# A written-out order for every instruction and place, and stacked one-pass state products for half of w_in

## The chip, the cores and the metric

The kernel runs on one core of one Trainium2 chip. The metric is the device time of one execution in microseconds (us); a smaller number is better. The core has five engines with their own queues, each of which works strictly in order: TensorE (PE; its weight loads are shown apart as PEld), VectorE (DVE), ScalarE (ACT), GpSimd (POOL) and SyncE (SP), which here only issues transfers. Matmul results land in PSUM, which has 8 banks of 128 x 512 float32; everything else lives in SBUF, or in DRAM.

## The reference

Eight batches (B) of 8 heads (H), 512 tokens (S), 32 state rows (NS), 64 columns per head (D). First a two-way attention between tokens and state, then a two-layer network with softplus over all rows of all batches (512 + 32 rows per batch, 512 model columns, 2048 hidden columns).

```python
scores = scale * np.matmul(x, state.transpose(0, 1, 3, 2))
a = softmax(scores)                 # with 1e-09 added to the sum
xread = np.matmul(a, state)
scores2 = scale * np.matmul(state, x.transpose(0, 1, 3, 2))
a2 = softmax(scores2)
sread = np.matmul(a2, x)
rows = np.concatenate([xread, sread], axis=2)     # heads side by side: 4608 rows of 512
...
h = rows @ w_in                     # 512 x 2048
g = np.maximum(h, 0.0) + np.log1p(np.exp(-np.abs(h)))
out = g @ w_out                     # 2048 x 512
```

w_in and w_out are float64; x, state and the output are float32.

## The kernel before

**Numbers in parts.** TensorE multiplies float32 in full, or float32r in one pass with fewer bits. Where the kernel uses float32r it splits a value into a high part (a cast, `split` L101, line L105 on ScalarE or L98 on GpSimd) and a low part (value minus high part, L106, on VectorE or GpSimd) and adds three products (PASSES: high x high, high x low, low x high). The float64 weights arrive as 64-bit words and are put together to float32 by `as_f32` (L120): a scaling of the upper words on ScalarE or GpSimd (L129 to L136), shifts of the lower words on VectorE (L131, or the 16-bit pair L140 and L141), and a join on VectorE (L142).

**The xread rows** are never formed. Since xread @ w_in = a @ (state @ w_in), the kernel multiplies the state of each batch with w_in first. w_in is cut into four quarters c of 512 hidden columns. This state product is V; V of one batch and quarter is 128 x 2 x 512. It is made in two ways:

- For batches 0 to 3 by `make_v0` (quarter 0, in 8 pieces of 256 columns) and `make_vf` (quarters 1 to 3, four pieces q of 512 columns each). Two float32 matmuls per piece, one with QZ[0] (batches 0 and 1; L185, L227) and one with QZ[1] (batches 2 and 3; L194, L238). The result for batches 0 and 1 is copied into SBUF tiles Vf (L232, L234); the one for batches 2 and 3 goes through a tile ve to DRAM (Vd[0, c]).
- For batches 4 to 7 by `make_v`: the converted w_in, which was stored to DRAM (wsc), is read back piece by piece; `head` (L271) stacks the high part of the 64 rows of a head over their low part into one 128 x 512 tile R; `product` (L259, matmuls in L262) multiplies it with the high and the low state parts (StK), two one-pass matmuls for the four batches at once. The result goes to DRAM (Vd[1, c], one page per head).

**The main loop.** A slot (b, ft) is batch b and hidden block ft of 128 columns, 16 per batch. `gemm1` (L506) makes h for it with six matmuls of 512 columns (L513) from V and the attention weights aT; `softplus` (L498) applies softplus on ScalarE (L500) and splits the result into ghi and glo; `gemm2` (L517) adds 4 x 3 matmuls (L520) into four accumulator banks. Every quarter of V is split before its use (`split_v`). Batches 0 and 1 take turns by quarters of ft (0: block 0 to 3; 1: 0 to 7; 0: 4 to 11; 1: 8 to 15; 0: 12 to 15), with partial sums kept in SBUF in between (L609, L612), so that work can begin before all of w_in and w_out is there. Then come batches 2 to 6, the state rows of all batches (`gemm1_read`, L560, from sreadT and w_in read back from DRAM), and batch 7.

**Attention** (`attention`) is a generator with one step per letter: scores (Q: L369 in float32 for batches 0 and 1, L375 for the others), VectorE's 32 x 32 transpose and the softmax over the state rows (A, M, m, N, D), the softmax over the tokens (E, e), the transposes on TensorE (G, L425), the reads (R: L443, L449), and the gathering into sr (X, L465 to L469).

**The order** is written by hand: LOADS for the first transfers, the strings START, BLOCK, BLOCK2, BLOCK3 and LAST for everything behind, one letter per step (`run`, L638): a bar is a gemm1 slot, g a gemm2, p a split of V, F a fetch of V, v, V and U a step of the three ways to make V, W a w_out block, a to c a step of attention. MOVED is a set of steps that run on another engine than usual; most of them are casts and differences that go to GpSimd. Tiles come from pools with a tag and a number of buffers; PSUM is divided into 2 banks "aux", 2 "h", 4 "acc".

All transfers are issued on SP's queue in the order of the program.

Of the kernel before, what the change touches and what calls it, by code (L numbers as in the profile page):

```python
# [49 lines left out]
def attention_then_softplus_mlp(ctx: ExitStack, tc, xn, xt, zq, zp, stk, w_in, w_out, out):  # L50
    nc = tc.nc
    nc.scalar.preload_act_table_set("natural_log_exp_and_others")

    cp = ctx.enter_context(tc.tile_pool(name="cp", bufs=1))
    sp = ctx.enter_context(tc.tile_pool(name="sp", bufs=1))
    dp = ctx.enter_context(tc.tile_pool(name="dp", bufs=1, space=DRAM))
    ps = ctx.enter_context(tc.tile_pool(name="ps", bufs=1, space=PSUM))
    uid = [0]

    def sb(tag, shape, dt=F32, bufs=1):  # L60
        uid[0] += 1
        return sp.tile(shape, dt, tag=tag, name=f"{tag}_{uid[0]}", bufs=bufs)

    def bank(tag, bufs):
        uid[0] += 1
        return ps.tile([P, 512], F32, tag=tag, name=f"{tag}_{uid[0]}", bufs=bufs)

    BANKS = {"aux": 2, "h": 2, "acc": 4}
    turn = cycle(("h", "acc", "acc"))
    early = [True]  # L70

    def aux():
        if early[0]:
            tag = next(turn)
            return bank(tag, BANKS[tag])
        return bank("aux", 2)

    ident = cp.tile([P, P], F32, name="ident")
    make_identity(nc, ident)


    if WARM:
        idle = sb("sr", [P, P], bufs=2)
        nc.vector.memset(idle, 0.0)
        pb = aux()
        for _ in range(WARM):
            nc.tensor.matmul(pb[:, 0:P], idle, idle, start=True, stop=True)

    def rouse():
        pb = aux()  # L90
        for c in range(4):
            nc.tensor.transpose(pb[:, P * c:P * c + P], ident, ident)

    def vec(*what):
        return nc.gpsimd if what in MOVED else nc.vector

    def pool_copy(dst, src):
        nc.gpsimd.tensor_scalar(dst, src, 1.0, 0.0, ALU.mult, ALU.add)  # L98


    def split(hi, lo, src, *what):  # L101
        if ("hi",) + what in MOVED:
            pool_copy(hi, src)
        else:
            nc.scalar.copy(hi, src)  # L105
        vec(*what).tensor_tensor(lo, src, f32(hi), ALU.subtract)  # L106

    def load_w(src, tag=None):
        w64 = src.dtype == I64
        tag = tag or ("k4" if w64 else "wt")  # L110
        t = sb(tag, src.shape, I64 if w64 else F32, bufs=K4 if tag == "k4" else 2)
        nc.sync.dma_start(t, src)
        return t

    def as_f32(t, *what, tag="wt"):  # L120
        if t.dtype != I64:
            return t
        v = t.bitcast(I32).rearrange("p (n t) -> p n t", t=2)
        lo, hi = v[:, :, 0], v[:, :, 1]
        n = t.shape[1]
        h2 = sb("k2", [P, n], bufs=K2)
        r = sb(tag, [P, n], bufs=2 if tag == "wt" else 1)
        if early[0] or ("pre",) + what in MOVED:
            nc.scalar.activation(h2, f32(hi), AF.Prelu, scale=2.0 ** -112, alpha=-(2.0 ** 32))  # L129
            u = r.bitcast(I32)  # L130
            nc.vector.tensor_scalar(u, lo, 29, None, ALU.logical_shift_right)  # L131
        else:
            if ("h2",) + what in MOVED:
                nc.gpsimd.tensor_scalar(h2, f32(hi), 2.0 ** -112, 0.0, ALU.mult, ALU.add)
            else:
# [205 lines left out]

# [404 lines left out]
```

## Time and profile before

| | |
|---|---|
| median of 3 runs | 697.95 us (695.63 to 699.69) |
| span of the profiled execution | 695.4 us |
| TensorE busy | 675.9 us, 3028 matmul records |
| VectorE busy | 395.0 us, 692 instructions |
| ScalarE busy | 390.9 us, 661 instructions |
| GpSimd busy | 218.4 us, 209 instructions |
| moved by DMA | 82.90 MB, mean 119 GB/s |

Engines are named PE, PEld, DVE, ACT, POOL and SP (SPq: its queue); L12 is line 12 of the kernel. In the view of groups, a row gives line, engine, operation, what is written from what, the matmul's shape of weights and of moving data, how many records; then busy time in us, mean ns of one, and the idle time just before them with what ended it. In the view by stretches, each engine has its busy time and the number of its instructions, followed by the granted TensorE clock, the share of the 16 DMA engines in use, and GB/s. In the timeline, a row begins with its start and its length in us; a row x12 is twelve instructions merged. A float32 matmul leaves two records, a one-pass one leaves one. In the view of transfers, the last number is the median time in us from issue to landing.

### The profile page before, as it was taken

To read this page: it belongs to the slowest core of one execution; us is meant where nothing else is said; L and a number is where in the kernel's file an instruction comes from. 1 tells how busy PE (TensorE), PEld (TensorE's weight loads), DVE (VectorE), ACT (ScalarE), POOL (GpSimd) and SP (SyncE) were. 2 spreads that over 40 slices of the span, in tenths; PEclk is the share of its full clock that TensorE was granted. 3 is DMA by queue.
4 is the path that set the end of the run, shared out by engine and by line. 5 is a ranking of instruction groups with operands and counts; after the bars stand their busy time and mean duration, and the time that the engine had idled before them with its cause. 6 is when DMAs were issued, how large, how long until landed. Compare 5 with 4: busy or idle time off the path is not lost.

```text
span 695.4 us, 8922 instructions
## 1 busy us (share of the span) xinstructions
PE 675.9 (97%) x3028; PEld 540.1 (78%) x3028; DVE 395.0 (57%) x692; ACT 390.9 (56%) x661; POOL 218.4 (31%) x209
## 2 busy tenths in 40 slices
PE   7879999999999999999999999999999999999997
PEld 4456667788887877888888888888888889988886
DVE  5898788319777885776556752676257423311101
ACT  4787975434848944775538634863386334423321
POOL 0130157146433584156222450235022400121310
PEclk9999999999999999999999999999999999999999
DMA  7778895103253545464423220321121113512001
GB/s 253 258 258 293 307 301 188 49 0 122 68 167 122 184 156 166 143 199 136 134 94 121 69 90 31 107 76 31 31 69 45 40 39 98 168 30 61 1 0 61
DMA packets 42061, 82.90 MB, mean 119 GB/s; under 512 B 6176, under 2 KB 13088, under 8 KB 42016
## 3 DMA queue, kind: packets, MB, share of 16 engines
q1 hardware_dynamic: 42016, 82.33, 36.1%
q8 instruction: 24, 0.39, 0.2%
q14 instruction: 21, 0.17, 0.1%
HBM read 56.62 MB, written 25.69 MB: 118 GB/s over the span
## 4 chain that ended last, share of the span: by engine, by line
PE 83%; ACT 7%; DVE 5%; DMA 2%; issue 1%; POOL 1%; SPq 0%; POOLq 0%; DVEq 0%; ACTq 0%
PE acc L520 49%; PE h L513 22%; PE h L560 3%; PE aux L262 2%; PE aux L449 2%; PE aux L375 1%; ACT L500 1%; DMA xT<-in_xt_dram 1%; ACT t L500 1%; PE aux L425 1%; PE aux L238 1%; PE aux L227 1%; DMA k<-in_w_in_dram 1%; ACT ghi L105 1%; DVE glo L106 1%
## 5 line engine op out<-in xcount | busy, mean ns | idle before, releaser
L520 PE MATMUL acc<-wout,ghi 128*128 128x512 f32 x1088 | 341.7, 395 | 3.9 <-POOL wout L98 2.8
L520 PEld LDWEIGHTS acc<-wout,ghi 128*128 128x128 f32 x1088 | 203.8, 189 | 50.7 <-issue 3.6
L520 PE MATMUL acc<-wout,glo 128*128 128x512 f32 x544 | 214.2, 394 | 0.0
L513 PE MATMUL h<-aT,vhl 128*128 128x512 f32 x768 | 199.4, 398 | 0.1
L513 PEld LDWEIGHTS h<-aT,vhl 128*128 128x128 f32 x768 | 142.1, 188 | 35.3 <-issue 3.4
L500 ACT ACTIVATE t<-h 128x512 f32<-128x512 f32 x136 | 81.0, 598 | 121.4 <-PE h L513 81.1
L106 DVE TENSOR_TENSOR glo<-t,ghi 128x512 fp32r<-128x512 f32 x83 | 63.7, 770 | 124.2 <-ACT ghi L105 83.9
L106 POOL TENSOR_TENSOR glo<-t,ghi 128x512 fp32r<-128x512 f32 x53 | 70.9, 1338 | 159.5 <-ACT ghi L105 156.7
L520 PEld LDWEIGHTS acc<-wout,glo 128*128 128x128 f32 x544 | 102.4, 188 | 23.0 <-issue 0.7
L105 ACT CAST ghi<-t 128x512 fp32r<-128x512 f32 x96 | 59.1, 618 | 76.1 <-PE acc L520 75.6
L106 DVE TENSOR_TENSOR vhl<-vf,vhl 128x512 fp32r<-128x512 f32 x57 | 41.5, 728 | 58.6 <-ACT vhl L105 48.4
L98 POOL TENSOR_SCALAR ghi<-t 128x512 fp32r<-128x512 f32 x40 | 28.7, 718 | 82.1 <-PE acc L520 39.5
L105 ACT CAST vhl<-vf 128x512 fp32r<-128x512 f32 x60 | 37.1, 618 | 17.3 <-PE h L513 11.3
L500 ACT ACT_TABLE_LOAD x23 | 29.5, 1283 | 7.8 <-DVE glo L106 5.7
L380 DVE TENSOR_TENSOR sc<-aux,k 64x512 f32<-64x512 f32 x24 | 16.4, 683 | 23.4 <-ACT k L379 23.1
L98 POOL TENSOR_SCALAR vhl<-vf 128x512 fp32r<-128x512 f32 x12 | 8.4, 696 | 66.8 <-PE h L513 50.7
L277 DVE TENSOR_TENSOR R<-wt,R 64x512 fp32r<-64x512 f32 x23 | 18.8, 819 | 10.4 <-ACT R L276 7.3
L560 PEld LDWEIGHTS h<-sreadT,vhl 128*128 128x128 f32 x192 | 24.1, 191 | 0.6
L560 PE MATMUL h<-sreadT,vhl 128*128 128x256 f32 x192 | 24.3, 283 | 0.0
L106 POOL TENSOR_TENSOR vhl<-vf,vhl 128x512 fp32r<-128x512 f32 x15 | 21.9, 1457 | 6.4 <-ACT vhl L105 6.0
L262 PE MATMUL aux<-R,StK 128*128 128x512 f32 x64 | 19.1, 398 | 1.2 <-POOL R L277 0.7
L398 POOL TENSOR_TENSOR T<-T,mx 128x512 f32<-128x512 f32 x7 | 7.7, 1106 | 37.3 <-DVE mx L397 17.4
(156 smaller groups left out, 736.3 us busy)
## 6 DMA issues: line engine op xcount, KB each, us to landing
vd<-ve SPq DMA_DIRECT2D x44, 256.0 KB, 2.7
xT<-in_xt_dram SPq DMA_DIRECT2D x16, 512.0 KB, 3.7
k<-in_w_out_dram SPq DMA_DIRECT2D x16, 512.0 KB, 5.1
x<-in_xn_dram SPq DMA_DIRECT2D x16, 512.0 KB, 3.5
vf<-vd SPq DMA_DIRECT2D x64, 128.0 KB, 2.6
k<-in_w_in_dram SPq DMA_DIRECT2D x12, 512.0 KB, 4.9
out_dram<-o SPq DMA_DIRECT2D x24, 256.0 KB, 2.2
vf<-vd SPq DMA_DIRECT2D x16, 256.0 KB, 4.0
```

The lines of the kernel that those rows point to most:

```text
L98: nc.gpsimd.tensor_scalar(dst, src, 1.0, 0.0, ALU.mult, ALU.add)
L105: nc.scalar.copy(hi, src)
L106: vec(*what).tensor_tensor(lo, src, f32(hi), ALU.subtract)
L262: nc.tensor.matmul(pb, StK[i][:, h, :], r, start=(i == 0), stop=(i == 1))
L277: vec("R", *what, o).tensor_tensor(r[z], wf[a], f32(r[a]), ALU.subtract)
L380: nc.vector.tensor_tensor(sc[64 * j:64 * j + 64], pb[0:64], s2, ALU.add)
L398: vec("tmul", bk, g).tensor_tensor(T, T, sm.unsqueeze(2).broadcast_to([P, 16, NS]), ALU.mult)
L449: nc.tensor.matmul(pb[:, 256 * j:256 * j + 256], a2T[:, c, j].rearrange("p i n -> p (i n)"), v["xs"][j][:, c].rearrange("p i n -> p (i n)" ...
L500: nc.scalar.activation(t, h, AF.Softplus)
L513: nc.tensor.matmul(h, Vhl[b, ft // 2][:, vi, g, cs], aT[b][:, ai, g], start=(n == 0), stop=(n == 5))
L520: nc.tensor.matmul(acc[c], g[gi][:, c0:c0 + P], wout[ft][:, wi], start=(ft == first and i == 0), stop=(ft == last and i == 2))
L560: nc.tensor.matmul(h[:, 256 * i:256 * i + 256], Whl[u, i][:, wi, kt, :], sreadT[:, si, kt, :], start=(n == 0), stop=(n == 11))
```

## The change

The generators, the order strings and MOVED are replaced. A function `graph` now names every step of the kernel as an operation with its inputs, its outputs and the engines that may run it; the string PLAN lists all 2638 steps in one order, each as name, engine and buffer numbers. T is TensorE, A ScalarE, V VectorE, G GpSimd, S an issue on SP's queue; C and W are the second forms of the two conversion steps (C: the plain scaling on ScalarE; W: the pair of 16-bit shifts on VectorE). A buffer number is a place in SBUF (69 places of 2 KB per partition, and a few of 4 KB) or one of the 8 PSUM banks, without fixed roles. Every engine gets its steps in the order of PLAN.

```diff
+TURNS = ((0, 0, 4), (1, 0, 8), (0, 4, 12), (1, 8, 16), (0, 12, 16))
+PACKED = (2, 3)
+
+PLAN = """
+Lz.0:S:0 Lt.0.1.0:S:1 Lt.0.1.1:S:2 zn.0:G:3 Li.0.1:S:4 Li.0.0:S:5 Lq.1:S:6 Lq.0:S:7 Li.0.6:S:8 Lt.0.0.0:S:9 zc.0.0:V: zc.0.1:V: Lt.0.0.1:S:10
...
+gl.0.1:V:24 m.0.0.2:T:1 wh.3:A:36 wl.2:V:20 m.0.1.0:T: gl.0.2:V:37 m.0.1.1:T: wl.3:V:28 m.0.2.0:T: m.1.1:A: gl.0.3:V:30 m.1.0:A: m.0.2.1:T: N.1.1:V:
...
+P.1.2.0:T:2 o.1.0.0:V:9 Sp.0.2.5:S: P.1.2.2:T:3 pe.1.2.0:V:25 m.1.7.3:T: pe.1.2.2:V:5 Sp.1.2.0:S: P.0.2.0:T:0 o.1.0.3:V:48 P.0.2.1:T:2 Sp.1.2.2:S:
...
+So.7.2:S: o.7.0.3:A:63 So.7.3:S:
+"""
...
+    def stack(c, h, o, src, tok):
+        a, z = slice(64 * o, 64 * o + 64), slice(64 - 64 * o, 128 - 64 * o)
+        R = f"R.{c}.{h}"
+        op(f"Rh.{c}.{h}", "AG", [tok], [f"{R}:h"], lambda e: copy(e, r(at(R)[a]), at(src)[a]))
+        op(f"Rl.{c}.{h}", "VG", [tok, f"{R}:h"], [f"{R}:l"],
+           lambda e: eng(e).tensor_tensor(r(at(R)[z]), at(src)[a], at(R)[a], ALU.subtract))
+        for s4 in range(2) if c in PACKED else (1,):
+            k = f"{s4}.{c}.{h}"
+
+            def product(e, k=k, s4=s4):
+                for i, s in enumerate(("KH", "KL")):
+                    mm(at(f"pp.{k}"), r(page(f"{s}.{s4}.{h // 4}", 4, P)[:, h % 4]), r(at(R)), i == 0, i == 1)
+
+            op(f"P.{k}", "T", [f"KH.{s4}.{h // 4}", f"KL.{s4}.{h // 4}", f"{R}:h", f"{R}:l"], [f"pp.{k}"], product)
+            op(f"pe.{k}", "AV", [f"pp.{k}"], [f"px.{k}"], lambda e, k=k: copy(e, at(f"px.{k}"), at(f"pp.{k}")))
+            store(f"Sp.{k}", [f"px.{k}"], lambda s4=s4: io.Vd[s4, c][h], lambda k=k: at(f"px.{k}"), [f"D:vd.{k}"])
...
+            if c in PACKED:
+                for o in range(2):
+                    stack(c, 2 * q + o, o, f"wf.{k}", wf)
+                continue
+            for z in range(2):
+                op(f"V{z}.{k}", "T", [f"QZ.{z}", wf], [f"vp.{z}.{k}"],
+                   lambda e, z=z, k=k, q=q, n=n: mm(at(f"vp.{z}.{k}")[:, 0:n], page(f"QZ.{z}", 4, P)[:, q],
+                                                    page(f"wf.{k}", n), True, True))
...
+                kept = b < WHOLE and c not in PACKED
...
+                    n = 4 if b >= 4 or c in PACKED else 2
...
+    with tc.manual_schedule():
...
+        ops = graph(io, at, nc)
+        for step in PLAN.split():
+            name, e, where = step.split(":")
+            step = ops.pop(name)
+            where = [int(w) for w in where.split(",") if w]
+            for buf in step.places():
+                if buf not in place:
+                    put(buf, where.pop(0))
+            assert not where
+            step.emit(e)
+        assert not ops
```

Three things differ in what is done, beside order and places:

- **State products of quarters 2 and 3.** For the quarters in PACKED the float32 products with QZ are gone. The stacks R (`stack`: Rh, Rl) are made from the converted piece directly, and for each head the product P is made twice, with the state of batches 0 to 3 (s4 = 0) and of batches 4 to 7 (s4 = 1). Both results are copied (pe), stored to DRAM (Sp), and fetched (F) by all eight batches; batches 0 and 1 no longer keep V of these quarters in SBUF. Two more pieces of the stacked state (Lk) are loaded and split (kh, kl). Quarters 0 and 1 are made as before.
- **Engines.** In PLAN, GpSimd has two steps (zn, a memset each). All casts are on ScalarE, all differences on VectorE.
- **Transfers.** V is fetched by half quarters (256 columns), in pieces of 64 KB, or 128 KB where batches 2 and 3 read quarters 0 and 1; xT is loaded in two pieces per group. There are 466 issues in PLAN.

Names of steps in PLAN used below: V0 and V1 are the float32 products with QZ, h.b.ft is a gemm1, m.b.ft.c one accumulator's share of a gemm2, P.s4.c.h a stacked product, Q the scores, G and T transposes, R.b.g the reads.

More of the change, by code (lines that the diff above doesn't have):

```diff
@@ L1 @@
 from contextlib import ExitStack
-from itertools import cycle
 import concourse.bass as bass
@@ new lines, in width, with rounded @@
+def width(buf):
+    kind, *at = buf.split(".")
+    whole = at and at[0] in map(str, range(WHOLE))
+    if kind in ("vp", "pp", "qp", "gp", "rp", "tp", "h", "acc") or kind == "sc" and whole:
+        return 0
+    if kind in ("o8", "x", "xs", "Wf", "Vk"):
+        return 2
+    return 2 if kind == "w8" and at[0] != "0" or kind == "aa" and not whole else 1
+def rounded(buf):
+    kind, *at = buf.split(".")
+    return kind in ("KH", "KL", "R", "Vh", "Vl", "aH", "aL", "xh", "xl", "xs", "Wh", "Wl", "gH", "gL", "uH", "uL") \
+        or kind in ("z", "aa") and int(at[0]) >= WHOLE
@@ L49, in attention_then_softplus_mlp @@
+SMALL = {"mx": 16, "sm": 16, "nm": 1, "rs": 1, "rj": 2}
+class IO:
+    pass
 @with_exitstack
@@ L68, in attention_then_softplus_mlp @@
[L68 to L76, printed above, removed]
-    ident = cp.tile([P, P], F32, name="ident")
[L79 to L85, printed above, removed]
-        for _ in range(WARM):
-            nc.tensor.matmul(pb[:, 0:P], idle, idle, start=True, stop=True)
@@ L89, in rouse @@
[L89 to L106, printed above, removed]
@@ L492, in split_wout @@
-    def split_wout(ft):
-        assert ft < NFT - 1 or all(made[0, c] == 3 for c in range(1, 4))
-        wout[ft] = sb(f"wout{ft}", [P, 2, DM], F32R)
-        w = as_f32(ahead("out"), ft)
-        split(wout[ft][:, 0], wout[ft][:, 1], w, "wout", ft)
-    def softplus(h, *what):
-        t = sb("t", [P, 512], bufs=2)
-        nc.scalar.activation(t, h, AF.Softplus)
-        ghi = sb("ghi", [P, 512], F32R, bufs=3)
-        glo = sb("glo", [P, 512], F32R, bufs=3)
-        split(ghi, glo, t, "g", *what)
-        return ghi, glo
@@ L506, in gemm1 @@
-    def gemm1(b, ft):
-        h = bank("h", 2)
-        n = 0
-        cs = slice(P * (ft % 2), P * (ft % 2) + P)
-        assert made["aT", b] == 2
-        for g in range(2):
-            for vi, ai in PASSES:
-                nc.tensor.matmul(h, Vhl[b, ft // 2][:, vi, g, cs], aT[b][:, ai, g], start=(n == 0), stop=(n == 5))
-                n += 1
-        return softplus(h, min(b, 4), ft)
-    def gemm2(acc, g, ft, cols, first=0, last=NFT - 1):
-        for c, c0 in enumerate(cols):
-            for i, (gi, wi) in enumerate(PASSES):
-                nc.tensor.matmul(acc[c], g[gi][:, c0:c0 + P], wout[ft][:, wi],
-                                 start=(ft == first and i == 0), stop=(ft == last and i == 2))
@@ L523, in store @@
-    def store(acc, dsts, tags="oooo"):
-        for a, d, tag in zip(acc, dsts, tags):
-            o = sb(tag, [P, DM], F32, bufs=2)
-            evac(o, a)
-            if len(d.shape) == 2:
-                nc.sync.dma_start(d, o)
-            else:
-                for i in range(4):
-                    nc.sync.dma_start(d[i], o[32 * i:32 * i + 32])
-    def chain(*gens):
-        for f in gens:
-            yield from f()
-    wv = [w.rearrange("(g j o d) f -> j d g o f", g=2, j=2, o=2) for w in wsc]
@@ L553, in gemm1_read @@
-    def gemm1_read(u):
-        assert made["read"] == B
-        h = bank("h", 2)
-        for i in range(2):
-            n = 0
-            for kt in range(4):
-                for wi, si in PASSES:
-                    nc.tensor.matmul(h[:, 256 * i:256 * i + 256], Whl[u, i][:, wi, kt, :], sreadT[:, si, kt, :],
-                                     start=(n == 0), stop=(n == 11))
-                    n += 1
-        return softplus(h, B, u)
-    COLS = [0, P, 2 * P, 3 * P]
-    QTR = NFT // 4
@@ L670, in attention_then_softplus_mlp @@
-    v0 = make_v0()
-    v_first = make_vf(range(1, 4))
-    v_second = chain(prep_stk, lambda: make_v(range(4), 2))
-    att[0] = attention(0, ATT[0])
-    n = 0
-    for what, i in LOADS:
-        if what == "w":
-            src = w_in[0, n % 4][:, 256 * (n // 4):256 * (n // 4) + 256]
-            first.append(load_w(src, ("k4", "k4", "R", "o")[n // 2]))
-            n += 1
-        elif what == "q":
-            nc.sync.dma_start(QZ[i], zq[:, i])
-        elif what == "z":
-            load_z(0)
-        else:
-            load_xT(0, i)
@@ L686, in attention_then_softplus_mlp @@
-    run(START)
-    assert made["read"] == 3
-    for b in range(2, B - 1):
-        run({2: BLOCK2, 3: BLOCK3}.get(b, BLOCK), b)
-    run("|gFp" * (NFT // 2))
-    run(LAST)
-    while pend:
-        flush(True)
+    io = IO()
+    io.xn, io.xt, io.zq, io.zp, io.stk, io.w_in, io.w_out, io.out = xn, xt, zq, zp, stk, w_in, w_out, out
+    io.wsc = [dp.tile([DM, 512], F32, tag=f"wsc{c}", name=f"wsc{c}") for c in range(4)]
+    io.Vd = {}
+    for c in range(4):
+        io.Vd[0, c] = dp.tile([H, P, 512] if c in PACKED else [P, 4, 512], F32, tag=f"vd0_{c}", name=f"vd0_{c}")
+        io.Vd[1, c] = dp.tile([H, P, 512], F32, tag=f"vd1_{c}", name=f"vd1_{c}")
@@ new lines, in attention_then_softplus_mlp, with put @@
+    ident = cp.tile([P, P], F32, name="ident")
+    sreadT = cp.tile([P, 2, 4, B * NS], F32R, name="sreadT")
+    fixed = {"ident": ident, "sreadT": sreadT.bitcast(F32)}
+    for n, w in SMALL.items():
+        t = cp.tile([P, 2 * B, w], F32, name=n)
+        for b in range(B):
+            for g in range(2):
+                fixed[f"{n}.{b}.{g}"] = t[:, 2 * b + g, :]
+    place = {}
+    def put(buf, i):
+        n = width(buf)
+        if n == 0:
+            place[buf] = ps.tile([P, 512], F32, tag=f"bank{i}", name=buf.replace(".", "_"), bufs=1)
+        else:
+            t = sp.tile([P, 512 * n], F32R if rounded(buf) else F32, tag=f"{'sd'[n - 1]}{i}", name=buf.replace(".", "_"), bufs=1)
+            place[buf] = t.bitcast(F32) if rounded(buf) else t
@@ new lines, in at @@
+    def at(buf):
+        return fixed[buf] if buf in fixed else place[buf]
+    with tc.manual_schedule():
+        make_identity(nc, ident)
+        put("idle", 0)
+        put("h.idle", 0)
+        nc.vector.memset(at("idle")[:, 0:P], 0.0)
+        for _ in range(WARM):
+            nc.tensor.matmul(at("h.idle")[:, 0:P], at("idle")[:, 0:P], at("idle")[:, 0:P], start=True, stop=True)
+        ops = graph(io, at, nc)
[9 more added lines that the diff above has]
+        assert not ops
```

1009 lines of the change are left out of this document (556 added, 453 removed).

## The prediction

> **What bounds the kernel now.** I read the page first, then the busy time by stretch, then the TensorE groups, then single stretches of the timeline for the time from one instruction to the next.
>
> ```profile
> span 695.4 us, 8922 instructions
> ...
> PE 675.9 (97%) x3028; PEld 540.1 (78%) x3028; DVE 395.0 (57%) x692; ACT 390.9 (56%) x661; POOL 218.4 (31%) x209
> ...
> PE 83%; ACT 7%; DVE 5%; DMA 2%; issue 1%; POOL 1%; SPq 0%; POOLq 0%; DVEq 0%; ACTq 0%
> ```
>
> TensorE is the bound. But a busy PE is not a PE at its peak: matmuls overlap, so I count its work by the time from one start to the next.
>
> ```profile
> 675.29 16.33 PE acc L520 x72
> ...
> 589.75 2.87 PE h L560 x24
> ```
>
> ```profile
> 84.28 1.02 PE L227 MATMUL aux<-wt,QZ 128*128 128x512 f32 x2
> 85.14 1.02 PE L238 MATMUL aux<-wt,wout 128*128 128x512 f32 x2
> 85.60 1.03 PE L520 MATMUL acc<-wout,ghi 128*128 128x512 f32 x2
> 86.46 0.40 PE L520 MATMUL acc<-wout,glo 128*128 128x512 f32 x1
> ```
>
> A one-pass 512-column matmul (float32r) takes 16.33 / 72 = 0.227 us. A full float32 one is two records; from 84.28 to 86.46 there are two of them and two one-pass matmuls, so one takes (2.18 - 0.45) / 2 = 0.863 us, 3.8 times as much.
>
> ```profile
> L520 PE MATMUL acc<-wout,ghi 128*128 128x512 f32 x1088 | 341.7, 395 | 3.9 <-POOL wout L98 2.8 <-ACT wout L105 1.0 <-DVE StK L612 0.2
> L520 PE MATMUL acc<-wout,glo 128*128 128x512 f32 x544 | 214.2, 394 | 0.0
> L513 PE MATMUL h<-aT,vhl 128*128 128x512 f32 x768 | 199.4, 398 | 0.1
> L560 PE MATMUL h<-sreadT,vhl 128*128 128x256 f32 x192 | 24.3, 283 | 0.0
> L262 PE MATMUL aux<-R,StK 128*128 128x512 f32 x64 | 19.1, 398 | 1.2 <-POOL R L277 0.7 <-DVE sreadT L106 0.6
> ...
> L375 PE MATMUL aux<-k,zhl 128*128 128x512 f32 x48 | 13.3, 392 | 0.1
> ...
> L185 PE MATMUL acc<-wt,QZ 128*128 128x256 f32 x2 | 0.6, 379 | 0.0
> ```
>
> The one-pass 512-column matmuls are 1088 + 544 + 768 + 64 + 48 = 2512, or 569.7 us; L560's 192 take 192 x 2.87 / 24 = 23.0. The other groups of this view, down to the last one shown, come by the same way to 62 us (24 products of w_in at 0.863 are 20.7 of it, the rest is attention and w_in's first quarter). The work is 654.8 us, so 40.6 us of the span are lost. Where:
>
> ```profile
> core 0: us, PE busy (x) PEld busy (x) DVE busy (x) ACT busy (x) POOL busy (x), PEclk, DMA share, GB/s
> ...
> 85.00:650.00 565.00, 562.14 (x2588) 458.95 (x2587) 323.29 (x534) 314.91 (x520) 200.32 (x186) 1.00 0.33 104
> 0.00:85.00 85.00, 72.13 (x260) 47.31 (x261) 64.81 (x149) 64.14 (x122) 11.05 (x16) 0.98 0.79 272
> 7.67:85.00 77.33, 65.73 (x241) 42.73 (x241) 64.64 (x148) 62.85 (x121) 9.88 (x9) 0.98 0.80 280
> ```
>
> ```profile
> L513 PE MATMUL h<-aT,vhl 128*128 128x512 f32 x54 | 16.3, 431 | 0.0
> L520 PE MATMUL acc<-wout,ghi 128*128 128x512 f32 x40 | 14.9, 452 | 3.8 <-POOL wout L98 2.8 <-ACT wout L105 1.0
> L520 PE MATMUL acc<-wout,glo 128*128 128x512 f32 x20 | 9.5, 474 | 0.0
> L369 PE MATMUL aux<-xT,Z 128*128 128x512 f32 x16 | 8.9, 683 | 3.8 <-DMA xT<-in_xt_dram 3.6 <-DMA Z<-in_zp_dram 0.2
> ...
> L425 PE MATMUL h<-ident,sc 128*128 128x128 f32 x4 | 0.7, 286 | 0.0
> ```
>
> This second view holds the first 85 us alone: 114 one-pass matmuls (25.9 us), and in float32 the 8 score matmuls (6.9), 13 w_in products (11.2), 16 of half the width (6.9), 16 reads (7.0) and the transposes (2.4): 60.3 us of work. So the opening loses 24.7 us. The last matmul ends at 675.29 + 16.33 = 691.6, so the tail is 3.8. The remaining 12.1 lie in 565 us: 2.9 of them as idle time, the others as matmuls that follow each other a little later than 0.227.
>
> **The change, part by part.** *State products.* For w_in's quarters 2 and 3 the 16 float32 products (V0, V1) go: 16 x 0.863 = 13.8 us. The stacked product of each head, two one-pass matmuls, which batches 4 to 7 have already (L262), is now also made for batches 0 to 3: 2 quarters x 8 heads x 2 = 32 matmuls, 32 x 0.227 = 7.3. TensorE wins 6.5 us, and at 97% busy I count it in full: 654.8 - 6.5 = 648.3. The stacks themselves are not new, they are built earlier and from the converted piece in place, without reading it back. Evacuations fall from 24 to 16, two splits of the state for batches 0 to 3 are added; off the path.
>
> *GpSimd emptied.* Its 218.4 us go; casts go to ScalarE, differences to VectorE. What they cost there, and what GpSimd costs VectorE now:
>
> ```profile
> 522.00 0.69 DVE L106 TENSOR_TENSOR k<-x,k 128x512 fp32r<-128x512 f32 x1
> 522.61 0.70 DVE L383 STREAM_TRANSPOSE T<-sc 128x512 f32<-128x512 f32 x1
> ...
> 539.80 2.42 DVE L468 TENSOR_TENSOR sr<-k 32x128 f32<-32x128 f32 x2
> ...
> 554.38 0.57 DVE L468 TENSOR_TENSOR sr<-k 32x128 f32<-32x128 f32 x2
> ```
>
> ```profile
> 64.63 0.45 DVE L141 TENSOR_SCALAR k<-k 128x512 uint16<-128x512 uint16 x1
> 64.97 0.45 DVE L140 TENSOR_SCALAR k<-k 128x512 uint16<-128x512 uint16 x1
> ```
>
> ```profile
> 539.48 2.60 POOL L106 TENSOR_TENSOR aT<-k,aT 128x512 fp32r<-128x512 f32 x2
> ```
>
> ```profile
> 626.58 0.61 ACT L105 CAST vhl<-vf 128x512 fp32r<-128x512 f32 x1
> 627.09 0.62 ACT L105 CAST ghi<-t 128x512 fp32r<-128x512 f32 x1
> ```
>
> Back to back, VectorE needs 0.61 us for 512 columns (0.34 for a 16-bit shift), ScalarE 0.51. The same pair of VectorE additions takes 2.42 us while GpSimd works from 539.48 to 542.08, and 0.57 with GpSimd idle: the two hold each other up. The Trainium skill says so too (SBUF — State Buffer, section Who interferes with whom): a VectorE instruction with two SBUF inputs shares a port with a GpSimd instruction that reads SBUF, and the later one waits in full; the two rows agree. By that page the whole list could run at the undisturbed prices, which is my upper end for VectorE and not my value.
>
> *The opening.* I cut it where the list has given TensorE the same 60.2 us of work, at the step m.1.4.0 (4 scores, 16 + 6 products, 2 transposes, 2 reads, 12 h and 30 m). Up to there the list holds for VectorE 73 steps of one 512-column pass (44.3 us at 0.61), 7 pairs of shifts (4.8), 22 shifts or half-width steps at 0.34 (7.5), and 16 short ones (6.6): 63.2 us.
>
> ```profile
> 7.67 0.29 DVE L131 TENSOR_SCALAR wout<-k 128x256 int32<-128x256 int32 x1 [6.67 <-DMA k<-in_w_in_dram]
> ```
>
> VectorE starts when the first piece of w_in has landed, now at 7.67, and as many bytes stand ahead of it in the new list. Never idle, it would be there at 70.9 (10.7 us lost). As full as it is now, 64.64 of 77.33 us, it needs 75.6 us and is there at 83.3 (23.1 lost). The transfers give a value between: the list issues 20.4 MB up to that step (66 transfers), which at the 272 GB/s of the first 85 us take 75.1 us, 14.9 lost. I take 14.9, since the DMA share of 0.79 says that the transfers are the scarcer thing; the ends stay in the range. The z, QZ and w_in pieces come in another order (both halves of QZ now ahead of most of w_in), which I count inside this number.
>
> *A new trip through DRAM.* Batches 0 and 1 now read quarters 2 and 3 from DRAM, as the others do.
>
> ```profile
> vd<-ve SPq DMA_DIRECT2D x44, 256.0 KB, 2.7
> ...
> vf<-vd SPq DMA_DIRECT2D x64, 128.0 KB, 2.6
> ```
>
> ```profile
> 280.69 0.32 SPq L285 DMA_DIRECT2D wt<-wsc  x1
> ```
>
> Between the last product of quarter 2 for batch 0 (P.0.2.1) and the first h that needs it (h.0.8) the list gives TensorE 16.3 us of other work. The trip is evacuation 0.6, store 2.7, fetch 2.6, cast and difference 0.5 + 0.6, and some 12 issues on SP's queue at 0.32: 11 us. It is hidden with 5 us to spare, so I count nothing. SP's queue stands still while a store waits for its evacuation; behind it stand the fetches of batch 1 and w_out loads. The fetches are now cut in pieces of 64 KB (192 of them). The Trainium skill (DMA: Bandwidth & Descriptors, section Measured) gives 0.95 us for 64 KB against 6.15 for 1 MB, a rule against this part; by it the 8 pieces of a quarter would take 7.6 us, an estimate from that page, and the trip would still fit. No run here shows it.
>
> *Order.* The blocks and turns keep their order; the last quarter of the last batch still ends in four evacuations and stores, so the tail stays at 3.8. For the stretch behind the opening I keep 12.1. Bounds: 4, if every visible wait and two thirds of the late matmuls go; 18, if VectorE and ScalarE, who take over 200 us of GpSimd's work there, add half.
>
> **Sum.** 648.3 + 14.9 + 12.1 + 3.8 = 679.1 us of span. The median of the three runs, 697.95, is 2.55 above the profiled span; with that, 681.6, taken as 682.0.
>
> **Rivals.** *The opening stays as it is* (24.7 lost). For it: TensorE waits there for xT and QZ, for loads, and every byte of w_in and w_out is still needed. Against it: the 11 us of POOL work that hold VectorE up go. It gives 648.3 + 24.7 + 12.1 + 3.8 + 2.55 = 691.4.
>
> *VectorE becomes the bound, slower than before.*
>
> ```profile
> L106 DVE TENSOR_TENSOR glo<-t,ghi 128x512 fp32r<-128x512 f32 x83 | 63.7, 770 | 124.2 <-ACT ghi L105 83.9 <-POOL ghi L98 38.3 <-POOL vhl L106 1.2
> ...
> L468 DVE TENSOR_TENSOR sr<-k 32x128 f32<-32x128 f32 x24 | 18.9, 787 | 0.3
> ```
>
> If GpSimd is not what makes these rows long, VectorE's steps cost their mean durations (0.77 where I took 0.61). Up to the step m.1.15.2, where TensorE has done 180.6 us, VectorE then has 190.9 us of work. At a fill of 0.836 as above it is there at 7.67 + 228.3 = 236.0; then come 467.7 of TensorE work, 6 lost behind it, the tail and 2.55: 716. It decides from a fill of 0.91 downward (698 there). Against it stand the two L468 rows.
>
> *The trip through DRAM is late.* If stores stuck in SP's queue make it 20 us instead of 11, TensorE waits 4 us at quarter 2 and about as much at quarter 3, each for batch 0 or 1: 690. For it: SP's queue is strictly in order. Against: in the list stores and fetches stand apart.
>
> **Chances.** Forecast 0.70; opening unchanged 0.12; late trip 0.08; VectorE bound 0.10. A measurement of this kernel tells about 0.5% (3.5 us) from no change. The forecast's whole span lies under 694.5; of the opening and the late trip, 0.12 fall under it and 0.08 within; of the VectorE case 0.01 within and 0.09 above. So faster 0.82, same 0.09, slower 0.09. The low end takes an opening of 10.7 and a middle near 4: 648.3 + 10.7 + 4 + 3.8 + 2.55 = 669.4; the high end takes in both middle rivals and a little more, 694.
>
> **What the new profile would show.** Right: no POOL work beside a few memsets; 32 more one-pass products and 16 fewer float32 ones; L468's successor (the gather into sr) at 0.28 each; 60 us of TensorE work done by about 75 us; the last 600 us packed. Wrong: TensorE waiting for VectorE differences or for fetched V pieces between 85 and 200 us (VectorE bound, late trip), or the first gemm2 still at 37 us (opening).

## The result and the profile after

The changed kernel takes 676.86 us (median of 4 runs, 675.82 to 677.97), the kernel before 697.39 in the same series: a ratio of 0.9708, 95% interval 0.9681 to 0.9735. The forecast was 682.0, range 669 to 694. The profiled execution took 675.82 us, 1.8 above its span.

From the page of the changed kernel: span, busy times, the engines' shares of the chain that ended last, and the group of the softplus differences.

```profile
span 674.0 us, 8950 instructions
...
PE 660.8 (98%) x3028; PEld 540.2 (80%) x3028; DVE 408.1 (61%) x790; ACT 420.9 (62%) x746; POOL 1.6 (0%) x8
...
PE 91%; DVE 4%; DMA 2%; ACT 2%; issue 1%; SPq 0%; ACTq 0%
...
L305 DVE TENSOR_TENSOR gL<-t,gH 128x512 fp32r<-128x512 f32 x136 | 92.3, 686 | 172.5 <-ACT gH L289 172.2
```

GpSimd's 218.4 us are gone, but VectorE is only 13.1 us busier than before: its 136 differences cost 0.686 us each, where 83 of them cost 0.770 before. The same by stretch:

```profile
42.00:85.00 43.00, 42.68 (x174) 32.01 (x174) 41.21 (x85) 39.30 (x68) 0.00 (x0) 1.00 0.52 186
85.00:650.00 565.00, 565.00 (x2653) 470.58 (x2652) 335.56 (x636) 346.54 (x607) 0.00 (x0) 1.00 0.36 112
0.00:85.00 85.00, 75.54 (x289) 53.18 (x290) 69.77 (x151) 67.31 (x129) 1.63 (x8) 1.00 0.69 248
```

From 85 to 650 us TensorE is never idle. Ahead of that it is VectorE that is hardly ever idle: from 42 to 85 us it works 41.21 of 43 us. The prediction's cut, the step m.1.4.0 with 60.2 us of TensorE work done, is the first three of these acc matmuls; the fourth begins the next step, so the cut lies at 78.64 (timeline of TensorE):

```profile
77.97 0.39 PE L308 MATMUL acc<-Wh,gH 128*128 128x512 f32 x1
78.19 0.39 PE L308 MATMUL acc<-Wl,gH 128*128 128x512 f32 x1
78.42 0.39 PE L308 MATMUL acc<-Wh,gL 128*128 128x512 f32 x1
78.64 0.39 PE L308 MATMUL acc<-Wh,gH 128*128 128x512 f32 x1
```

And its last matmuls, from the chain of waits (start, length):

```profile
662.09 8.17 PE acc L308 x36
```

They end at 670.26, so the tail is 3.7. The prediction's sum with what came: work 648.3, opening 78.64 - 60.2 = 18.4 (forecast 14.9), tail 3.7 (3.8), and what is left of 674.0 for the middle, 3.6 (12.1). Two terms were mis-sized, in opposite directions.

Why the opening is longer than forecast shows on SP's queue and VectorE. The first issue in the changed kernel, then VectorE's first conversion of w_in:

```profile
4.87 0.38 SPq L296 DMA_DIRECT2D zf<-in_zp_dram  x1
```

```profile
12.03 0.50 DVE L337 TENSOR_SCALAR wf<-w 128x256 int32<-128x256 int32 x2 [4.54 <-DMA w<-in_w_in_dram]
```

The first transfer of the program is issued at 4.87 us, and VectorE's first conversion begins at 12.03 where the kernel before had it at 7.67. The list puts the tile of that transfer (zf.0) in place 0; ahead of the list, the kernel puts the tile that the eight warm-up matmuls read (idle) in place 0 too. The first load therefore waits until the warm-up is over (its 16 matmul records run from 1.05 to 4.85 us), and so does everything behind it in SP's queue.

### The profile page after: what moved, and what is told of

It reads as the page before. It is cut to its first block, busy times and chain, and to the rows that moved or that the text cites. A ratio compares the mean times of both kernels' runs of the same rounds, so it can differ in the third digit from the quotient of the medians.

```text
span 674.0 us, 8950 instructions
## 1 busy us (share of the span) xinstructions
PE 660.8 (98%) x3028; PEld 540.2 (80%) x3028; DVE 408.1 (61%) x790; ACT 420.9 (62%) x746; POOL 1.6 (0%) x8
## 4 chain that ended last, share of the span: by engine, by line
PE 91%; DVE 4%; DMA 2%; ACT 2%; issue 1%; SPq 0%; ACTq 0%
PE acc L308 53%; PE h L308 28%; PE pp L308 3%; PE rp L308 3%; PE qp L308 2%; PE gp L494 1%; DMA vd<-ve 1%; DMA w<-in_w_in_dram 1%; PE vp L308 1%; DVE wf L345 1%; PE h_idle L768 1%; DVE gL L305 1%; PE sc L308 1%; ACT Vk L289 0%; DVE Vl L305 0%
## 5 line engine op out<-in xcount | busy, mean ns | idle before, releaser
L308 PE MATMUL acc<-Wh,gH 128*128 128x512 f32 x544 | 215.3, 396 | 0.0
L308 PE MATMUL acc<-Wh,gL 128*128 128x512 f32 x544 | 212.1, 390 | 0.1
L308 PE MATMUL acc<-Wl,gH 128*128 128x512 f32 x544 | 212.1, 390 | 0.0
L305 DVE TENSOR_TENSOR gL<-t,gH 128x512 fp32r<-128x512 f32 x136 | 92.3, 686 | 172.5 <-ACT gH L289 172.2
L308 PEld LDWEIGHTS acc<-Wh,gL 128*128 128x128 f32 x544 | 102.1, 188 | 22.8 <-DVE gL L305 1.2
L308 PEld LDWEIGHTS acc<-Wl,gH 128*128 128x128 f32 x544 | 102.2, 188 | 21.2 <-issue 0.9
L308 PEld LDWEIGHTS acc<-Wh,gH 128*128 128x128 f32 x544 | 102.2, 188 | 21.1 <-issue 0.7
L308 PE MATMUL h<-aH,Vh 128*128 128x512 f32 x256 | 101.9, 398 | 0.2 <-ACT Vh L289 0.2
L308 PE MATMUL h<-aH,Vl 128*128 128x512 f32 x256 | 99.9, 390 | 0.1
L308 PE MATMUL h<-aL,Vh 128*128 128x512 f32 x256 | 99.8, 390 | 0.1
```

The lines of the kernel that those rows point to most:

```text
L305: lambda e: eng(e).tensor_tensor(r(dlo()), src(), dhi(), ALU.subtract))
L308: nc.tensor.matmul(dst, lhs, rhs, start=start, stop=stop)
```

## The experiments

Each run is compared with runs of the kernel before on the same chip (medians there 697.03, 697.51 and 697.2 in the three series); a ratio is to those. The changed kernel and e1 were each measured in one series only, so a difference between runs of two series can be off by the half us by which these medians differ.

**e1: the idle tile elsewhere.**

```diff
-        put("idle", 0)
+        put("idle", 68)
```

> The changed kernel with one number changed: the tile of zeros for the eight warm-up matmuls lies in place 68 and no longer in place 0, which the first transfer (z of batch 0) writes. In the changed kernel's trace SP issues that transfer at 4.87 us, when the warm-up matmuls have ended; in the kernel before it issues its first at 0.74. Theory (the first loads bound the start of the opening): everything behind moves up by the 4.1 us, 672 to 673 us against the changed kernel's 676.9. Rival (the opening is bound by VectorE's work or by the sum of the bytes, so that a start 4 us earlier is eaten before step m.1.4.0): 675.5 to 677.

Measured 671.76 (671.10 to 672.69), ratio 0.9645 (0.9625 to 0.9664): 5.1 us less than the changed kernel, 4.7 in the profiled spans. The first issue is now at 0.74, 4.13 earlier, and m.1.4.0 ends at 73.99, 4.65 earlier:

```profile
0.74 0.38 SPq L297 DMA_DIRECT2D zf<-in_zp_dram  x1
```

```profile
73.99 0.39 PE L309 MATMUL acc<-Wh,gH 128*128 128x512 f32 x1
```

The late start is real and costs its whole length. This is the fastest version found, and the base of e5 to e12.

**e2: the price of the products.** The product for batches 0 to 3 as one full float32 matmul, in place of two one-pass ones (the low part of the state is left out of it):

```diff
+                if s4 == 0:
+                    mm(at(f"pp.{k}"), page(f"KH.{s4}.{h // 4}", 4, P)[:, h % 4], at(R), True, True)
+                    return
```

> The changed kernel, but the 16 stacked products for batches 0 to 3 (P.0.2.h and P.0.3.h) are one full float32 matmul instead of two one-pass ones, without the low part of the state, so the values are not the reference's; the price on TensorE is that of the products that the change took out, 0.863 us instead of 0.453, with every copy, store and fetch as in the changed kernel. Theory (TensorE bound there, its work counts in full): 16 x 0.41 = 6.6 us more, 683.5. Rival (these products lie in a stretch in which TensorE has slack, and the gain came from elsewhere): below 679.

Measured 682.46, ratio 0.9797 (0.9779 to 0.9815): 5.6 us more than the changed kernel, for 16 x (0.863 - 0.454) = 6.5 us of TensorE work. Work on TensorE counts nearly in full.

**e3: casts and differences back on GpSimd, in the new order.** Behind m.1.4.0, the 184 steps that GpSimd had in the kernel before:

```diff
-gl.1.5:V:29
+gl.1.5:G:29
```

(and so on; that line stands for 184 changes of the engine's letter.)

> The changed kernel in the same order and places, but behind step m.1.4.0 the 184 casts and differences that the kernel before had on GpSimd are on GpSimd again. Theory (emptying GpSimd is what made the stretch behind the opening 7 us shorter: GpSimd and VectorE no longer hold each other up): 682 to 686, with VectorE's differences at about 0.77 us instead of 0.686. Rival (the written-out order did it, GpSimd is neutral): 676 to 678.5.

Measured 689.73, ratio 0.9903 (0.9879 to 0.9926): 12.9 us more than the changed kernel, above what was expected. VectorE's differences, then GpSimd's:

```profile
L306 DVE TENSOR_TENSOR gL<-t,gH 128x512 fp32r<-128x512 f32 x85 | 67.8, 809 | 136.3 <-ACT gH L290 73.9 <-POOL gH L292 62.3
```

```profile
L306 POOL TENSOR_TENSOR gL<-t,gH 128x512 fp32r<-128x512 f32 x51 | 68.3, 1340 | 242.5 <-ACT gH L290 206.2 <-DMA Vf<-vd 11.9 <-issue 11.0
```

```profile
85.00:650.00 565.00, 557.00 (x2596) 460.09 (x2595) 323.17 (x540) 301.75 (x522) 199.85 (x176) 1.00 0.35 112
```

VectorE's difference goes from 0.686 to 0.809, GpSimd's takes 1.340, and TensorE has 8.0 us of idle time from 85 to 650 us where it had none. That leaves two causes: the engines hold each other up, or TensorE waits for the slower of the two. The longest of TensorE's waits in that stretch (total, times, longest):

```profile
PE h L309 <- POOL Vl L306: 3.2, 2, 2.5
PE acc L309 <- DVE gL L306: 1.7, 1, 1.7
PE acc L309 <- POOL gL L306: 1.5, 2, 1.3
```

Of all the waits of this view, 5.6 us are for results of GpSimd and 2.2 for results of VectorE. So late results of GpSimd are the larger part of what shows as waiting; how much of their lateness comes from VectorE beside them is not shown. e5 asks whether the first cause can cost time at all.

**e4: GpSimd emptied in the old order.**

```diff
-MOVED = {('R', 1, 0, 3, 0), ('R', 1, 0, 3, 1), ...}
+MOVED = {m for m in MOVED if m[0] in ('pre', 'v0', 'vd', 've', 'sr', 'a2T')}
```

> The kernel before with its own order, but without GpSimd: every cast, scaling and difference that its set MOVED sends to GpSimd runs on ScalarE or VectorE. Theory (GpSimd held VectorE up and cost the stretch behind the opening about 7 us and the opening a few more): 686 to 692 against 697.4. Rival (GpSimd is neutral, the order is what counts, and this order was made for GpSimd's help): 697 or slower.

Measured 694.09, ratio 0.996 (0.9945 to 0.9974): only 2.9 us less than the kernel before. It lies between the two numbers on record, 2 us above the theory's 686 to 692. The stretch behind 85 us, then the opening:

```profile
85.00:650.00 565.00, 564.50 (x2602) 461.70 (x2601) 343.18 (x638) 372.91 (x616) 0.00 (x0) 1.00 0.32 103
0.00:85.00 85.00, 71.20 (x261) 47.06 (x262) 65.55 (x152) 65.81 (x126) 1.17 (x7) 0.98 0.84 281
```

The opening does as much as before (261 matmul records to 260), and the middle goes from 12.1 to about 692.3 - 654.8 - 24.7 - 3.8 = 9.0. With e3 this makes a table of four (the lower row has the cheaper products too, 6.5 us of work; its left entry has GpSimd busy behind the opening only):

| | GpSimd with casts and differences | GpSimd empty |
|---|---|---|
| old order | 697.0 | 694.1 |
| order written out | 689.7 | 676.9 |

Emptying GpSimd is worth 2.9 us in the old order and 12.9 in the new one. But the old order was written for GpSimd's help and the new one for its absence, so each entry with the other's division of the work has an order that was not made for it. The table shows that the gain belongs to the two together; it does not show what an order written out with GpSimd's help would have reached.

**e5, e9, e10: GpSimd work beside, for which nobody waits.** 184 instructions on a scrap tile, from m.1.4.0 on; only the instruction differs:

```diff
+            ops[f"dg{i}"] = Op(f"dg{i}", "G", [], [], lambda e: nc.gpsimd.tensor_tensor(scrap[0], scrap[0], scrap[0], ALU.subtract))
```

(e9: `nc.gpsimd.memset(scrap[0], 0.0)`; e10: `nc.gpsimd.tensor_scalar(scrap[0], scrap[0], 1.0, 0.0, ALU.mult, ALU.add)`.)

> On top of the kernel with the idle tile in place 68 (671.76): 184 subtractions of 128 x 512 on a scrap tile of their own, on GpSimd, from the step m.1.4.0 on; nothing waits for them. They make GpSimd as busy as the casts and differences did that cost 12.9 us when they stood there (GpSimd's own work there was 205 us, 1.34 us for one subtraction). Theory (the two engines hold each other up when both read SBUF; VectorE's 0.69 us grow to 0.81 and more, and the fixed order has no slack for it): 6 to 13 us more, 678 to 685. Rival (what cost time was only that TensorE waited for results that GpSimd makes in 1.34 instead of 0.69 us, in an order written for VectorE): within 2 us of 671.8.

> On top of the kernel with the idle tile in place 68 (671.76): as in the run with 184 subtractions beside (751.4), but the 184 GpSimd instructions are memsets of the same scrap tile, which read nothing. Theory (VectorE and GpSimd shut each other out when both read SBUF; a write alone does not): within 2 us of 671.8, though GpSimd works some 100 us (184 x 0.53). Rival (any GpSimd work beside costs VectorE or its queue about its own length): 20 us more or above.

> On top of the kernel with the idle tile in place 68 (671.76): the same with 184 one-input copies (the form that casts had on GpSimd, 0.74 us there). If one input is enough to shut VectorE out: the 184 x 0.74 = 136 us of GpSimd work hold VectorE up for a part of that, and TensorE is late by 20 to 60 us (690 to 730). If only two inputs do so: within 3 us of 671.8. The theory so far does not tell which; the first fits the rule that both must read.

| beside | GpSimd busy, one | time | ratio |
|---|---|---|---|
| nothing (e1) | | 671.76 | 0.9645 (0.9625 to 0.9664) |
| e5, subtractions | 233.7 us, 1.27 | 751.40 | 1.0777 (1.0746 to 1.0807) |
| e10, copies | 151.7 us, 0.82 | 698.37 | 1.0019 (0.9999 to 1.0039) |
| e9, memsets | 100.8 us, 0.55 | 675.17 | 0.9680 (0.9652 to 0.9707) |

Work for which nobody waits costs up to 79.6 us, far above the 678 to 685 on record for e5: the engines hold each other up, and the rival (late results alone) would have given 671.8. But e5 is not e3: its 184 instructions run back to back from 73 to 320 us, while e3's lie scattered over 565 us. How e3's 12.9 us divide between this and GpSimd's late results was not measured. VectorE's timeline in e5, then GpSimd's in the same stretch:

```profile
198.89 1.52 DVE L316 TENSOR_TENSOR Wl<-ow,Wh 128x512 fp32r<-128x512 f32 x1
200.34 1.52 DVE L316 TENSOR_TENSOR xl<-xT,xh 128x512 fp32r<-128x512 f32 x1
201.79 1.52 DVE L316 TENSOR_TENSOR gL<-t,gH 128x512 fp32r<-128x512 f32 x1
```

```profile
199.95 7.15 POOL L789 TENSOR_TENSOR scrap<-scrap 128x512 f32<-128x512 f32 x5
```

One VectorE difference starts every 1.45 us in place of 0.60, one GpSimd subtraction every 1.43: they take strict turns here, and each subtraction holds VectorE up by 0.85 us. Not all of VectorE's work suffers (groups of e5, 80 to 320 us; count, busy, mean):

```profile
L316 DVE TENSOR_TENSOR gL<-t,gH 128x512 fp32r<-128x512 f32 x32 | 40.5, 1280 | 10.1 <-ACT gH L300 9.9
...
L304 DVE COPY px<-pp 128x512 f32<-128x512 f32 x22 | 14.8, 682 | 5.3 <-PE pp L319 4.8 <-PE acc L319 0.4
...
L464 DVE STREAM_TRANSPOSE T<-sc 128x512 f32<-128x512 f32 x3 | 2.1, 697 | 0.0
```

Copies out of PSUM and transposes stay at 0.68 and 0.70 (in e1 0.69 and 0.70). The Trainium skill (SBUF — State Buffer, section Who interferes with whom) says just this: VectorE with two SBUF inputs contends with GpSimd instructions that read SBUF, and not with those that only write; with one input it doesn't, except in its modes that use two ports, which `tensor_scalar` can enter. In e9 the differences keep their 0.69, and the shifts, `tensor_scalar` with one input, pay (e9, then e1, 80 to 170 us):

```profile
L316 DVE TENSOR_TENSOR gL<-t,gH 128x512 fp32r<-128x512 f32 x14 | 9.5, 688 | 5.8 <-ACT gH L300 5.7
...
L352 DVE TENSOR_SCALAR ow<-o 128x512 uint16<-128x512 uint16 x4 | 3.1, 775 | 0.0
```

```profile
L342 DVE TENSOR_SCALAR ow<-o 128x512 uint16<-128x512 uint16 x4 | 1.8, 451 | 0.0
```

The rows agree with the page in the first three points. The fourth fits, but no view tells in which mode a shift ran. e9 is 3.4 us slower than e1, where its theory had at most 2; the two intervals overlap a little. In e9 the shifts of this stretch take 4.7 us longer together, and TensorE waits 3.0 us between 73 and 330 us, most of it for a difference (none in e1):

```profile
PE acc L319 <- DVE gL L316: 2.0, 4, 0.8
```

That the shifts alone make the 3.4 us is likely and not shown. e10 lies between, in the range of 690 to 730 on record: copies read with one input, and hold VectorE up for a shorter time each.

**e6, e7, e8: what sets the pace of the opening.** Eight joins on VectorE issued twice (they leave their result as it is); eight stores of 256 KB more among the loads; the eight differences wl.0 to wl.7 on GpSimd:

```diff
+            if name in ('cr.o1', 'cr.o2', 'cr.o3', 'cr.o4', 'cr.o5', 'cr.o6', 'cr.o7', 'cr.1.0'):
+                step.emit(e)
```

```diff
+            ops[f"Sx{i}"] = Op(f"Sx{i}", "S", [], [], lambda e, i=i, copy=copy: nc.sync.dma_start(copy, at(f"QZ.{i % 2}")))
```

```diff
-wl.0:V:14
+wl.0:G:14
```

> On top of the kernel with the idle tile in place 68 (671.76): eight of the joins (cr.o1 to cr.o7 and cr.1.0) are issued twice in a row, which leaves their result as it is and adds 8 x 0.60 = 4.8 us of VectorE work between 28 and 66 us. Theory (VectorE sets the pace of the opening behind 28 us, where it is 93 to 96% busy): 3 to 5 us more, 674.8 to 676.8. Rival (the transfers set it, and VectorE waits in their shadow): under 1 us more.

> On top of the kernel with the idle tile in place 68 (671.76): eight stores of 256 KB more in SP's queue among the loads of w_out and w_in in the opening, from QZ to a scrap tensor in DRAM that nobody reads; 2.1 MB, 5.2 us at the 407 GB/s of 25 to 42 us. Theory of the prediction (the transfers are the scarcer thing in the opening): 3 to 5 us more, 674.8 to 676.8. Rival (VectorE sets the pace, the transfers have some 20 us of slack behind 42 us): under 1 us more.

> On top of the kernel with the idle tile in place 68 (671.76): the eight differences wl.0 to wl.7 of the opening on GpSimd instead of VectorE, order and places as they are. Theory (VectorE is the bound between 28 and 66 us, so 8 x 0.60 us taken off it are worth most of that): 2 to 4 us less, 668 to 670. Rival (GpSimd's 1.34 us for one, and VectorE held up meanwhile, eat the gain): within 1 us or up to 3 more.

e6: 676.89, ratio 0.9711 (0.9676 to 0.9747), 5.1 us more for 4.8 us of VectorE work. e7: 671.61, ratio 0.9632 (0.9611 to 0.9653), no change for 2.1 MB. The stretch 42 to 62 us in e1, then in e7:

```profile
42.00:62.00 20.00, 20.00 (x79) 14.41 (x77) 19.09 (x42) 16.42 (x30) 0.00 (x0) 1.00 0.56 192
```

```profile
42.00:62.00 20.00, 20.00 (x79) 14.61 (x78) 19.76 (x44) 16.43 (x30) 0.00 (x0) 1.00 0.82 295
```

The extra bytes raise the DMA share from 0.56 to 0.82 and the time stays. So behind 28 us, where e6 adds its work, VectorE sets the pace, and the transfers behind the first extra store don't:

```profile
21.47 0.32 SPq L773 DMA_DIRECT2D copy<-QZ  x1
```

Ahead of that nothing but the start was tried: e1 shows that a late first load costs its whole length, and e1's chain of waits still runs through three loads from 16.3 to 35.9 us:

```profile
16.32 6.35 DMA xT<-in_xt_dram
22.68 9.00 DMA w<-in_w_in_dram
31.70 4.21 DMA w<-in_w_in_dram
```

e8: 674.52, ratio 0.9672 (0.9652 to 0.9693), 2.8 us more: 4.8 us were taken off VectorE, but GpSimd took 1.595 us for each difference, and TensorE waited for VectorE's gL instead:

```profile
L306 POOL TENSOR_TENSOR Wl<-ow,Wh 128x512 fp32r<-128x512 f32 x8 | 12.7, 1595 | 56.2 <-ACT Wh L290 55.7 <-POOL Wl L306 0.4
```

```profile
PE acc L309 <- DVE gL L306: 2.5, 3, 1.3
```

**e11: four copies of the opening on ScalarE.**

```diff
-ve.0.2:V:23
+ve.0.2:A:23
```

(the same for o.0.0.3, ve.1.1 and va.1.1.0)

> On top of the kernel with the idle tile in place 68 (671.76): four copies out of PSUM that VectorE makes between 54 and 58 us (ve.0.2, ve.1.1, va.1.1.0, o.0.0.3; 2.4 us together) go to ScalarE. Theory (VectorE is the bound of the opening up to 66 us; 4.8 us more work there cost 5.1 us): 1 to 2.4 us less, 669.4 to 670.8. Rival (ScalarE, 7.9 of 8 us busy from 58 to 66, is the bound next to it, and the four only change places): within 0.7 us or slower.

Measured 673.44, ratio 0.9656 (0.9633 to 0.9679), which cannot be told from e1. There is no gain: TensorE now waits for a cast on ScalarE instead (1.4 us, 0.2 in e1), which is the bound right behind VectorE.

```profile
PE h L309 <- ACT Vh L290: 1.4, 1, 1.4
```

**e12: the trip through DRAM made longer.** Sixteen small stores in SP's queue between the last store of quarter 2 and its fetches:

```diff
+            ops[f"Sy{i}"] = Op(f"Sy{i}", "S", [], [], lambda e, spare=spare: nc.sync.dma_start(spare, at("ident")[:, 0:32]))
```

> On top of the kernel with the idle tile in place 68 (671.76): 16 more small stores (16 KB each, to scrap in DRAM) in SP's queue right behind the store of the last product of quarter 2 for batch 0 (Sp.0.2.1), ahead of the fetches that read it; they hold the queue up by 16 x 0.38 = 6 us. Theory of the prediction (the trip through DRAM has 5 us to spare): 0 to 2 us more. Rival (no slack, as the cast of the fetched piece already waits 1 us for the transfer): the 6 us come through whole, 676 to 678.

Measured 676.61, ratio 0.971 (0.9682 to 0.9739): 4.9 us more than e1, 3.2 in the profiled executions (spans 672.5 and 669.3). By the numbers on record that lies nearer the rival. The stores kept SP's queue for 9.08 us and not 6, but not all of that is delay: in e1 the queue waits 4.4 us at this place for V's last store to land. The first fetch is issued at 112.66, against 107.46 in e1. ScalarE's first cast of a fetched piece, which waits for the transfer in both, starts 5.2 us later (SP's timeline of e12, then of e1; the cast in e12, then in e1):

```profile
103.53 9.08 SPq L774 DMA_DIRECT2D spare<-ident  x16
112.66 2.31 SPq L298 DMA_DIRECT2D Vf<-vd  x5
```

```profile
107.46 2.21 SPq L297 DMA_DIRECT2D Vf<-vd  x5
```

```profile
115.68 0.62 ACT L291 CAST Vh<-Vf 128x512 fp32r<-128x512 f32 x1 [5.71 <-DMA Vf<-vd]
```

```profile
110.51 0.62 ACT L290 CAST Vh<-Vf 128x512 fp32r<-128x512 f32 x1 [0.99 <-DMA Vf<-vd]
```

TensorE's first product with a fetched piece (e12, then e1) comes 2.7 us later:

```profile
120.00 0.39 PE L310 MATMUL h<-aH,Vh 128*128 128x512 f32 x1
```

```profile
117.33 0.39 PE L309 MATMUL h<-aH,Vh 128*128 128x512 f32 x1
```

So of 5.2 us by which the pieces arrive later, 2.5 stay hidden by these rows, 2.0 by the profiled spans and 0.3 by the medians. TensorE does not wait for the piece itself: it waits 2.53 us for a copy out of PSUM on VectorE, which stands behind a result of ScalarE, which stands behind the cast.

## Why the prediction was right or wrong

**State products: right.** 6.5 us were counted in full; e2 gives back 5.6 of them.

**The opening: the range held, the reason failed.** The step "I take 14.9, since the DMA share of 0.79 says that the transfers are the scarcer thing" is wrong for what lies behind 28 us: 2.1 MB more cost nothing (e7), 4.8 us of VectorE work more cost 5.1 (e6). VectorE's own bound was the better one. In e1 it reaches m.1.4.0 after 62.8 us of work in the 65.9 us from 7.43 to 73.31; the 63.2 us counted from the list agree, and its fill is 0.95, not 0.836. With that fill the prediction's sum for VectorE gives 7.67 + 63.2 / 0.95 = 74.2. That opening loses 73.99 - 60.2 = 13.8, so the 14.9 lay near it by luck. What in the new order raised the fill was not taken apart. The 4.6 us above it come from the line "VectorE starts when the first piece of w_in has landed, now at 7.67, and as many bytes stand ahead of it": the bytes were counted, the place into which the first of them goes was not.

**The middle: the mis-sized term.** "For the stretch behind the opening I keep 12.1" became 3.6, just outside the bounds of 4 to 18. (By its own words, all 2.9 us of waits and two thirds of the other 9.2 gone, the lower bound comes to 3.1.) The two L468 rows, which the prediction had as the price of GpSimd's work beside VectorE, were used for VectorE's prices and not for TensorE's waits. In the new order, e3 puts 12.9 us back by GpSimd's work alone. But e4 shows that emptying GpSimd is not enough: in the old order the middle stays near 9.0. What part of the written-out order brings it from there to 3.6 was not taken apart.

**The errors nearly cancel.** +3.5 for the opening, -8.5 for the middle, and 1.8 instead of 2.55 between span and run, make 681.6 into 675.8. That the forecast lies only 5 us off is partly luck.

**The trip through DRAM: rightly counted as nothing, with less to spare than thought.** TensorE waits for no fetched V in the changed kernel. But where the prediction had 5 us to spare, e12 leaves 2.5 at most: the rival of the late trip did not come, and stood nearer than it looked.

**The rivals.** The opening did not stay as it was (18.4 lost, before 24.7). Its sign, though, was a bad one: the first gemm2 comes at 38.14, hardly moved, and the gain lies behind it. VectorE did not become the bound of the whole, as its differences take 0.686 and not 0.770; but of 42 to 85 us it is the bound, and e5 (751) shows how far disturbed prices on VectorE can move the whole. The prediction says that this rival decides from a fill of 0.91 downward; by its own sum it passes the forecast from 0.98 (7.67 + 190.9 / 0.98 + 467.7 + 6 + 3.8 + 2.55 = 682.5), and at 0.91 nothing of the gain is left.

## What to carry to other kernels

GpSimd's time beside VectorE is not free, even where nobody waits for its results: look for the same VectorE instruction with GpSimd busy and idle, and price it by the difference. When an order and its places are written out, look first at the first instruction of every queue and what it waits for: here one shared place cost about 5 us. To find what sets the pace of a stretch, give each candidate some idle work (a join twice, stores that nobody reads) and see which one costs its length.

## What the runs showed of the hardware

In e5 the granted TensorE clock fell while TensorE had to wait (73 to 150 and 150 to 300 us), though it is 1.00 in both stretches of e1; the last three columns are clock, DMA share and GB/s:

```profile
73.00:150.00 77.00, 57.79 (x218) 42.41 (x218) 66.99 (x70) 39.70 (x69) 72.45 (x59) 0.89 0.45 154
150.00:300.00 150.00, 119.43 (x457) 90.11 (x458) 138.65 (x153) 76.66 (x130) 141.37 (x111) 0.91 0.34 111
```

Gaps and a lower clock came together; no run here shows which brings which. TensorE is idle for 49.8 us of these 227 us, so a part of e5's 79.6 us may be the clock's.
